# Attention and two mixtures of experts on one core: a reordered front, gate weights through memory, key sums from added chunks, zero-padded small groups

## The chip, the cores and the metric

The kernel runs on one core of a Trainium2 chip. The metric is the device time of one execution in microseconds (us), as the median of several runs. The engines are named as in the profile: PE (TensorE matmuls), PEld (its weight loads), DVE (VectorE), ACT (ScalarE), POOL (GpSimd) and SP (SyncE, which here issues most of the DMAs).

## What is computed

Three layers follow each other. B = 4 batches of S = 576 tokens give 2304 tokens of width 512.

```python
def _attn_ref(q, k, v):                       # (4, 8, 576, 64)
    q_s = softmax of q over the 64 features
    k_s = softmax of k over the 576 tokens
    kv = np.einsum('bhsd,bhse->bhde', k_s, v)
    return np.einsum('bhsd,bhde->bhse', q_s, kv)

def _moe_ref(x, w_gate, w1, w2, capacity):    # 8 experts, 512 -> 1024 -> 512
    probs = softmax(x @ w_gate); expert = argmax; gate_w = probs[expert]
    # the first `capacity` tokens of each expert are kept
    out = gate_w * (relu(x @ w1[expert]) @ w2[expert])   # 0 for dropped tokens

def _moe2_ref(x, w_skip, w_gate, w1, w2):
    # only tokens with x @ w_skip > 0; same top-1 expert, no capacity
    out = x + gate_w * (relu(x @ w1[e]) @ w2[e])         # others: out = x
```

The kernel is laid out for data in which a batch's tokens go to one expert in a layer, or only a few of them to one or two others; the fourth batch lies beyond the experts' capacity and its output is zeros (word `Z`). A general path for other data stands behind a branch at the end and is not taken.

## The kernel before, in words

**Groups.** A *group* is one dense pass of an expert over the 576 tokens of a batch. There are five: (layer 0, batch 0), (0, 1), (0, 2), (1, 0), (1, 1), called groups 1 to 5 here. In a group the tokens stand as columns. A group has 16 *steps*, counted 0 to 15. Steps 0 to 7 make the hidden layer: 24 matmuls of 288 columns each (line 813), where every fp32 operand is split in a high and a low fp32r part (`split`, lines 753 on ACT and 754 on DVE), so that a product is three matmuls. ACT and DVE take each step's result out (`evacuate`, `hh` on line 847 and `hl` on line 848). Steps 8 to 15 make the output in pairs of steps (line 834); after an odd step DVE multiplies the result with `mg` (lines 863 or 866 and 867), a tile that holds the gate weight of each token in every partition. Two pairs of PSUM banks alternate, so that a step's products go on while the step before is taken out.

**The plan.** The table `COURSE` gives each step of each group one line of words: those ahead of the bar are written behind the step's products and the split of the weights of the step after next, then comes `evacuate` of the step, then the words behind the bar. All engines run their instructions in the order in which the program writes them (`manual_schedule`), so the table sets the order on every engine. The words:

- `c.` to `i.`: the halves (four heads each) of the attention of batches 1 to 3. `ld` loads q, k and v; `qm`, `q1` to `q3`, `qn` are the softmax of q; `km`, `kt`, `kc`, `ke` shift the keys by their column maxima and take exp; `kv` (lines 415 and 424) is k times v; `qt`, `re`, `rw` turn q and write the layer's input.
- `C` and `M`: the routing of the two layers (`g` guesses the expert from a token, so that weights can be loaded early; 1 to 6 are logits, one-hot, positions, counts and gate weights).
- `G.1` makes the gate weight of each token with three small DVE operations (lines 876 to 880) in a column layout `gm` (128 x 5). `G.2` (`gate2`, line 887) spreads it over all partitions: five matmuls with `gm` as broadcast weights against the identity, and two ACT copies (895, 897) into `mg`.
- `L` and `N` load the weights of this and the next group (line 771, `ws`), `X` splits the next group's input.
- `S` (layer 0, batch 2, one expert) and `T` (layer 1, batch 2, two experts) are the *small groups*: at most 32 tokens that go to another expert. `p`, `g`, `gx` gather them, `t` (`expert`, line 1083) multiplies by that expert's weights, which come in eight tiles `tw` through three buffers (the load of tile i + 3 is written behind the matmuls that read tile i), `v` and `a` make the placing matrix, `u` (`put`, line 1132) adds the result to the batch's tokens, with a lhsT of 64 partitions.
- `O` turns a finished piece of 128 columns and stores it.

**v in the halves.** For halves `c` to `i` the tile of v is 65 wide with a column of ones, so that the k sums come out of the same matmuls; it is loaded head by head (five DMAs a half). For the two halves `a` and `b` of batch 0 v is 64 wide, loaded with two DMAs, and the sums are matmuls of their own (line 424).

**The front.** The attention of batch 0 (`a`, `b`) runs ahead of the groups. Filler matmuls (`warm_up`, line 511, 95 in all, 46 of them at the start) stand between its steps on PE. The order is: k of both halves, k times v, the last 64 tokens of q through to `X[0]`, the guess of the expert from them, the first weight loads (`first.load`), the other 512 tokens, the splits, and `first_products` (line 792), the products of steps 0 and 1 of group 1.

## Time and profile before

| | us |
|---|---|
| median of 3 runs | 438.97 |
| the runs | 434.55, 441.33, 438.97 |
| the profiled execution | 437.39 |
| its span, first to last instruction | 435.6 |
| TensorE clock granted, mean over the span | 0.983 of full speed |

The span is what the trace shows; the 1.8 us beside it lie around it. A row of the trace gives start and duration in us, engine, line, operation and tiles. L813 is line 813 of the kernel. In a chain of waits each piece is what the next one waited for. PEclk is the granted clock: 1.00 is 2.4 GHz, 0.50 is 1.2 GHz.

### The profile page before, as it was taken

The numbers are of one execution on the slowest core, as the hardware profiler recorded it, in microseconds if no ns is written. First come the engines' busy times: TensorE is split into PE (matmuls) and PEld (weight loads), VectorE is DVE, ScalarE is ACT, GpSimd is POOL, SyncE is SP. The second block draws the span as 40 slices with busy tenths as digits, with TensorE's granted clock in tenths as the row PEclk, the third lists the DMA queues.
The fourth block names the chain that finished last, engine by engine and source line by source line (L and its number), as shares of the span: only waits on it lengthen the run. The fifth ranks groups of instructions, "written<-read, shape, count | busy, mean of one in ns | idle before, by whom it ended". The sixth has DMA issues, their size and how long they took to land.

```text
span 435.6 us, 8703 instructions
## 1 busy us (share of the span) xinstructions
PE 407.3 (94%) x3370; PEld 359.7 (83%) x3370; DVE 243.2 (56%) x623; ACT 188.2 (43%) x574; POOL 7.6 (2%) x34
## 2 busy tenths in 40 slices
PE   8999799999999999999999979998999989999993
PEld 4666689898999898999998769798998878888882
DVE  3776478463778642577364625477665433554441
ACT  4646756733278653333366131333473423222121
POOL 3000000000000000000000000000000000000000
PEclk9999899999999999999999989999999989999997
DMA  8909915201942000791516921131326595620133
GB/s 213 247 14 263 234 50 161 53 2 52 295 109 87 12 2 2 250 204 50 185 58 212 246 94 50 50 94 52 120 93 188 177 289 165 186 117 2 32 105 85
DMA packets 75087, 53.30 MB, mean 122 GB/s; under 512 B 22562, under 2 KB 70178, under 8 KB 75042
## 3 DMA queue, kind: packets, MB, share of 16 engines
q1 hardware_dynamic: 73088, 52.41, 41.7%
q10 hardware_dynamic: 1954, 0.31, 0.5%
q8 instruction: 27, 0.44, 0.4%
q14 instruction: 18, 0.15, 0.1%
HBM read 47.98 MB, written 4.72 MB: 121 GB/s over the span
## 4 chain that ended last, share of the span: by engine, by line
PE 77%; DVE 9%; ACT 5%; SPq 3%; DMA 2%; issue 2%; DVEq 0%; ACTq 0%
PE pair L834 26%; PE pair L813 24%; PE pair L511 3%; PE pk L415 3%; DMA tw<-in_moe_w_dram 2%; PE pxs L1027 2%; PE px L473 2%; PE pl L565 2%; SPq L283 2%; PE pg L887 2%; PE pair L792 1%; PE pts L1132 1%; PE ptq L444 1%; PE pto L1165 1%; PE ph L1083 1%
## 5 line engine op out<-in xcount | busy, mean ns | idle before, releaser
L834 PE MATMUL pair<-hh,wh 128*128 128x288 f32 x320 | 98.5, 308 | 0.0
L834 PE MATMUL pair<-hl,wh 128*128 128x288 f32 x320 | 94.6, 295 | 0.0
L834 PE MATMUL pair<-hh,wl 128*128 128x288 f32 x320 | 94.3, 295 | 0.0
L813 PE MATMUL pair<-xh,wh 128*128 128x288 f32 x304 | 94.2, 310 | 0.0
L813 PE MATMUL pair<-xl,wh 128*128 128x288 f32 x304 | 90.8, 299 | 0.0
L813 PE MATMUL pair<-xh,wl 128*128 128x288 f32 x304 | 90.6, 298 | 0.0
L754 DVE TENSOR_TENSOR wl<-ws,wh 128x512 fp32r<-128x512 f32 x80 | 54.8, 686 | 43.0 <-ACT wh L753 42.6
L847 ACT ACTIVATE hh<-pair 128x576 fp32r<-128x576 f32 x40 | 25.9, 648 | 91.9 <-PE pair L813 81.4
L834 PEld LDWEIGHTS pair<-hh,wh 128*128 128x128 f32 x320 | 60.5, 189 | 3.6 <-issue 1.7
L813 PEld LDWEIGHTS pair<-xh,wh 128*128 128x128 f32 x304 | 58.2, 192 | 2.8 <-issue 1.1
L834 PEld LDWEIGHTS pair<-hl,wh 128*128 128x128 f32 x320 | 60.5, 189 | 0.1
L834 PEld LDWEIGHTS pair<-hh,wl 128*128 128x128 f32 x320 | 60.4, 189 | 0.0
L813 PEld LDWEIGHTS pair<-xl,wh 128*128 128x128 f32 x304 | 58.4, 192 | 0.1
L813 PEld LDWEIGHTS pair<-xh,wl 128*128 128x128 f32 x304 | 58.3, 192 | 0.0
L848 DVE SCALAR_TENSOR_TENSOR hl<-pair,hh 128x576 fp32r<-128x576 f32 x40 | 30.2, 756 | 48.0 <-ACT hh L847 46.4
L332 ACT ACTIVATE eq<-qt,mx 128x64 f32<-128x64 f32 x152 | 50.7, 337 | 5.0 <-DVE mx L321 4.6
L753 ACT CAST wh<-ws 128x512 fp32r<-128x512 f32 x80 | 49.3, 620 | 4.2 <-PE pair L834 2.8
L332 ACT ACTIVATION_READ_ACCUMULATOR eq<-qt,mx 128x1 f32 x152 | 28.8, 190 | 0.0
L511 PE MATMUL pair<-warm 128*128 128x384 f16 x95 | 20.9, 366 | 1.6 <-DVE warm L903 1.6
L754 DVE TENSOR_TENSOR xl<-x,xh 128x576 fp32r<-128x576 f32 x20 | 15.1, 753 | 11.1 <-ACT xh L753 11.1
L1166 ACT COPY ot<-pto 128x256 f32<-128x256 f32 (+1 forms) x24 | 7.2, 316 | 31.7 <-PE pto L1165 31.6
L511 PEld LDWEIGHTS <-warm 128*128 128x128 f16 x95 | 10.0, 108 | 10.4 <-issue 5.5
(186 smaller groups left out, 505.2 us busy)
## 6 DMA issues: line engine op xcount, KB each, us to landing
ws<-in_moe_w_dram SPq DMA_DIRECT2D x39, 512.0 KB, 3.9
tw<-in_moe_w_dram SPq DMA_DIRECT2D x24, 512.0 KB, 4.8
qt<-in_q_dram SPq DMA_DIRECT2D x8, 512.0 KB, 6.6
kt<-in_k_dram SPq DMA_DIRECT2D x8, 512.0 KB, 7.6
vt<-in_v_dram SPq DMA_DIRECT2D x24, 128.0 KB, 6.1
out_dram<-ot SPq DMA_DIRECT2D x12, 256.0 KB, 2.9
out_dram<-zt SPq DMA_DIRECT2D x2, 576.0 KB, 7.2
vt<-in_v_dram SPq DMA_DIRECT2D x2, 512.0 KB, 6.9
```

The costliest lines, as they stand in the source:

```text
L283: nc.sync.dma_start(out=t[:, h, 0:4, 0:D], in_=s[h, 0:4 * P].rearrange("h (p j) d -> p h j d", j=4))
L332: nc.scalar.activation(self.eqv[:, h, j], self.qt[:, h, j], AF.Exp, bias=self.mx[:, i:i + 1], accum_out=self.qz[:, i:i + 1])
L415: nc.tensor.matmul(out=pk[64 * g:64 * g + 64, c * D1:c * D1 + w], lhsT=self.kt[:rows(j), 2 * c + g, j], rhs=self.vt[:rows(j), 2 * c + g, j ...
L473: nc.tensor.matmul(out=pt, lhsT=self.kd[:, c], rhs=self.qT[:, c, 0:4 * P], start=True, stop=True)
L511: nc.tensor.matmul(out=pw[:, 0, :3 * P], lhsT=warm16[:, 0:P], rhs=warm16, start=True, stop=True)
L565: nc.tensor.matmul(out=pl[32 * c:32 * c + 32, :HT], lhsT=self.weights[:, c], rhs=self.chunk(c, tokens(a)), start=True, stop=True,)
L753: nc.scalar.copy(hi, src)
L754: nc.vector.tensor_tensor(out=lo, in0=src, in1=hi.bitcast(F32), op=ALU.subtract)
L813: nc.tensor.matmul(out=self.pt[:, a, :HT], lhsT=u[:, c], rhs=w[:, c, tokens(a)], start=(c == 0 and n == 0), stop=(c == NC - 1 and n == 2),)
L834: nc.tensor.matmul(out=self.pt[:, a, :HT], lhsT=p_[:, f], rhs=w[:, tokens(a)], start=(v == 0 and f == 0 and n == 0), stop=(v == 1 and f == ...
L847: nc.scalar.activation(halves(hh), src, AF.Relu)
L848: nc.vector.scalar_tensor_tensor(out=halves(hl), in0=src, scalar=0.0, in1=halves(hh).bitcast(F32), op0=ALU.max, op1=ALU.subtract,)
```

## The change

**Front.** 34 fillers at the start in place of 46, and 54 in all in place of 95. Half `a`'s main tokens are normalized, turned and multiplied earlier; the last tokens of both halves go through one bank and one copy; the loop over halves at the end is written out, without fillers, and `set_capacity` (a tiny matmul `pcap` behind a DVE cast of the capacity) moves from group 1 to just ahead of `first_products`.

**Gate weights.** For groups 2 to 5 `G.1` now also turns `gm` to 5 x 128 on PE, copies it out on DVE and writes it to memory with a DMA; `G.2` reads it back into all 128 partitions with a second DMA. Group 1 keeps the old way in one word, `G.0`. In the plan `G.1` moves to the words behind the bar of step 3 (groups 2 and 3) or step 4 (groups 4 and 5).

**k sums.** Halves `g` and `i` (batch 3) have v 64 wide, loaded with two DMAs in place of five. A new word `kz` adds the five chunks of k on DVE (three operations); in `kv` two PE transposes and a DVE reduction turn that into the sums.

**Small groups.** `put` takes a zero-padded lhsT of 128 partitions; two words `u` do what four did. In the plan the words of `S` and `T` start a line earlier and `t04` stands two lines behind `t03`, where it stood one.

The guess uses one token, not 64.

```diff
-    e.ke f.qm |
+    e.ke f.qm | G.1
-    f.q2 G.1 | f.kc
+    f.q2 | f.kc
-    N2 g.qn | S.t03
-    X2 | S.t04 g.qt
+    N2 g.qn S.v0 | S.t03
+    X2 | S.a0 g.qt
+    N3 | S.t04
...
+        def kz(self):
+            s2 = self.tile([P, HH, 2, D], "s2", "m2")
+            s1 = self.tile([P, HH, D], "s1", "m1")
+            kt = self.kt
+            nc.vector.tensor_add(s2, kt[:, :, 0:2], kt[:, :, 2:4])
+            nc.vector.tensor_add(s1, s2[:, :, 0], s2[:, :, 1])
+            nc.vector.tensor_add(s1, s1, kt[:, :, 4])
...
         def gate1(self):
+            self.gate_weights()
+            pt = bank("pgm")
+            nc.tensor.transpose(pt[0:NJ, 0:P], self.gm, ident)
+            gT = rp.tile([NJ, P], F32, name="gT", tag="gT")
+            nc.vector.tensor_copy(out=gT, in_=pt[0:NJ, 0:P])
+            self.gd = dp.tile([NJ, P], F32, name="gate", tag="gate", bufs=2)
+            nc.sync.dma_start(out=self.gd, in_=gT)
         def gate2(self):
             self.mg = hp.tile([P, S], F32, name="mg", tag="mg")
+            src = self.gd.rearrange("j p -> (j p)")[0:S].rearrange("(o n) -> o n", o=1)
+            nc.sync.dma_start(out=self.mg, in_=src.to_broadcast([P, S]))
...
-        warm_up(46)
+        warm_up(34)
...
+        first.split_w(0)
+        x_out(b, 1)()
+        first.split_w(1)
+        set_capacity()
         first.early = first.first_products()
...
-                        lhsT=u[sl, (c % 2) * P:(c % 2 + 1) * P],
-                        rhs=self.pT[t][sl, tokens(a)],
+                            out=pt[:, :HT], lhsT=u[:, c], rhs=self.pT[t][:, tokens(a)], start=(n == 0), stop=(n == 1)
```

How instructions move. DVE at the end of the front (`xl`, `wl` are the low parts of the input and the weights), before:

```order
L365 TENSOR_TENSOR eq<-eq,qz 128x2x4x64
L754 TENSOR_TENSOR xl<-x_121,xh 128x576 x2
L754 TENSOR_TENSOR wl_206<-ws_198,wh_202 128x512
L754 TENSOR_TENSOR wl_207<-ws_198,wh_203 128x512
L754 TENSOR_TENSOR xl<-x_121,xh 128x576 x2
L754 TENSOR_TENSOR wl_208<-ws_199,wh_204 128x512
```

and in the changed kernel:

```order
L367 TENSOR_TENSOR eq<-eq,qz 128x2x4x64
L775 TENSOR_TENSOR xl<-x_121,xh 128x576 x3
L775 TENSOR_TENSOR wl_206<-ws_198,wh_202 128x512
L775 TENSOR_TENSOR xl<-x_121,xh 128x576
L775 TENSOR_TENSOR wl_207<-ws_198,wh_203 128x512
L248 CAST capf<-capi 1x1
L251 COPY rem<-pcap 128x8
L775 TENSOR_TENSOR wl_208<-ws_199,wh_204 128x512
```

The cast `capf`, on which the matmul `pcap` waits ahead of all products, now stands behind the last split of the front.

DVE in group 2 around step 3 (`hl` is the result of steps 2 and 3, `mx<-qt` the word `f.qm`), before:

```order
L848 SCALAR_TENSOR_TENSOR hl<-pair_83,hh 128x576
L400 TENSOR_TENSOR kt<-kt,pmax 128x1280
L754 TENSOR_TENSOR wl_207<-ws_200,wh_203 128x512
L318 TENSOR_REDUCE mx<-qt 128x20
L321 TENSOR_SCALAR mx<-mx 128x20
L848 SCALAR_TENSOR_TENSOR hl<-pair_84,hh 128x576
L754 TENSOR_TENSOR wl_208<-ws_201,wh_204 128x512
```

and in the changed kernel:

```order
L869 SCALAR_TENSOR_TENSOR hl<-pair_84,hh 128x576
L404 TENSOR_TENSOR kt<-kt,pmax 128x1280
L775 TENSOR_TENSOR wl_207<-ws_200,wh_203 128x512
L320 TENSOR_REDUCE mx<-qt 128x20
L323 TENSOR_SCALAR mx<-mx 128x20
L869 SCALAR_TENSOR_TENSOR hl<-pair_83,hh 128x576
L897 TENSOR_SCALAR hi<-dlo_137 128x1
L898 SCALAR_TENSOR_TENSOR gm<-z_135,dlo_137,gw_136 128x5
L901 SCALAR_TENSOR_TENSOR gm<-z_135,hi,gm 128x5
L909 COPY gT<-pgm 5x128
L775 TENSOR_TENSOR wl_208<-ws_201,wh_204 128x512
```

PE at the same place, between the last products of step 3 and the first of step 4, in the changed kernel:

```order
L834 MATMUL pair_83<-xl,wh_205 128x288
L834 MATMUL pair_83<-xh,wl_209 128x288
L907 MATMUL pgm<-c_85,gm 5x128
L834 MATMUL pair_84<-xh,wh_202 128x288
L834 MATMUL pair_84<-xl,wh_202 128x288
```

The three `gm` operations stand behind `hl` of the step that has just ended, and the transposing matmul that reads `gm` stands ahead of the next step's products, where before one step followed the other.

SP in group 3, from the load of half `i` to the small group's last weight tile, before:

```order
L286 DMA kt<-in_k_dram 64x4x64
L283 DMA vt<-in_v_dram 128x4x64 x4
L286 DMA vt<-in_v_dram 64x4x64
L771 ISA
L771 DMA ws_200<-in_moe_w_dram 128x4x256
L1063 ISA
L1063 DMA tw<-in_moe_w_dram 128x2x512
```

and in the changed kernel:

```order
L287 DMA kt<-in_k_dram 64x4x64
L284 DMA vt<-in_v_dram 128x4x256
L287 DMA vt<-in_v_dram 64x4x64
L792 ISA
L792 DMA ws_200<-in_moe_w_dram 128x4x256
L1120 ISA
L1120 DMA tw<-in_moe_w_dram 128x2x512
```

Three issues fewer stand ahead of `tw`.

## Rows read from the trace of the kernel before

**Rows 1.** The page, part 1: busy time of each engine, its share, its instructions

```profile
PE 407.3 (94%) x3370; PEld 359.7 (83%) x3370; DVE 243.2 (56%) x623; ACT 188.2 (43%) x574; POOL 7.6 (2%) x34
```

**Rows 2.** Waits of PE: us in total, times, longest

```profile
PE py L1083 <- DMA tw<-in_moe_w_dram: 4.5, 2, 3.4
PE pt L384 <- ACT eq L332: 3.1, 1, 3.1
PE pts L1132 <- DVE x L1140: 2.2, 3, 1.0
```

**Rows 3.** Chain in order of time, front into group 1: start, us, what

```profile
39.63 6.37 PE pair L792 x48
...
50.95 4.72 PE pair L813 x24
```

**Rows 4.** Windows: busy us of each engine, then PEclk, DMA share, GB/s

```profile
50.00:55.00 5.00, 4.46 (x24) 4.49 (x25) 2.51 (x5) 3.79 (x19) 0.00 (x0) 0.69 0.77 208
...
355.00:360.00 5.00, 4.54 (x24) 4.40 (x23) 1.20 (x3) 1.07 (x3) 0.00 (x0) 0.66 0.92 306
```

**Rows 5.** Timeline of the front: start, us, engine, line

```profile
1.55 10.59 PE L511 MATMUL pair<-warm 128*128 128x384 f16 x46 [1.55 <-DVE warm L903]
...
9.49 0.42 DVE L378 TENSOR_TENSOR m<-m,kt 128x256 f32<-128x256 f32 x1
...
30.04 0.15 DVE L556 TENSOR_SCALAR gid<-gid 64x1 int32<-64x1 int32 x1
...
30.93 0.98 SPq L771 DMA_DIRECT2D ws<-in_moe_w_dram  x2
```

**Rows 6.** Groups of instructions by form, ACT: busy us, mean ns

```profile
L753 ACT CAST xh<-x 128x576 fp32r<-128x576 f32 x20 | 13.5, 674 | 0.1
...
L987 ACT COPY x<-px 128x512 f32<-128x512 f32 x4 | 2.3, 583 | 1.5 <-PE px L473 1.5
```

**Rows 7.** Chain in order of time, group 2, products of steps 2 to 4

```profile
124.21 3.19 PE pair L813 x24
...
127.84 6.37 PE pair L813 x48
```

**Rows 8.** Timeline of DVE and PE: group 2 step 3, group 3 step 3, group 4 step 4

```profile
132.19 1.48 DVE L318 TENSOR_REDUCE mx<-qt 128x20 f32<-128x1280 f32 x1
...
133.78 0.75 DVE L848 SCALAR_TENSOR_TENSOR hl<-pair,hh 128x576 fp32r<-128x576 f32 x1
...
203.60 0.64 PE L1042 MATMUL ptx<-c,x 128*128 128x128 f32 x4
203.67 0.76 DVE L848 SCALAR_TENSOR_TENSOR hl<-pair,hh 128x576 fp32r<-128x576 f32 x1 [1.32 <-ACT hh L847]
...
289.61 0.76 DVE L848 SCALAR_TENSOR_TENSOR hl<-pair,hh 128x576 fp32r<-128x576 f32 x1 [0.51 <-ACT hh L847]
```

**Rows 9.** Groups of instructions by form, DVE: the last gate operation

```profile
L880 DVE SCALAR_TENSOR_TENSOR gm<-z,hi,gm 128x5 f32<-128x5 f32 x5 | 1.1, 225 | 0.2
```

**Rows 10.** Chain in order of time, group 3, steps 8 to 14

```profile
225.18 1.25 PE pg L887 x10
...
239.87 1.87 SPq L283
...
247.88 4.92 DMA tw<-in_moe_w_dram
...
255.80 3.67 PE pair L834 x24
```

**Rows 11.** Chain in order of time, group 5

```profile
348.20 5.89 DMA tw<-in_moe_w_dram
...
356.54 4.51 PE pair L813 x24
...
386.96 0.53 PE pts L1132 x2
...
390.86 0.99 PE pts L1132 x6
```

More of the change, by code (lines that the diff above doesn't have):

```diff
@@ L242 @@
     beyond_i = cp.tile([P, 1], I32, name="beyond_i")
-    gkey = [cp.tile([LAST, 1], F32, name=f"gkey{b}") for b in range(len(GUESS))]
-    gid = [cp.tile([LAST, 1], I32, name=f"gid{b}") for b in range(len(GUESS))]
+    gkey = [cp.tile([1, 1], F32, name=f"gkey{b}") for b in range(len(GUESS))]
+    gid = [cp.tile([1, 1], I32, name=f"gid{b}") for b in range(len(GUESS))]
     def set_capacity():
@@ L298, in load_v @@
         def load_v(self):
[L300 to L301 removed]
+            if self.sums == 0:
+                self.vt = self.big("vt", D1)
                 nc.gpsimd.memset(self.vt[:, :, :, D:D1], 1.0)
+            else:
+                self.vt = self.big("vt")
             self.load(v, self.vt)
@@ L926 @@
         a.ke()
-        warm_up(8)
+        warm_up(7)
+        b.kc_max()
         a.inverse()
         a.norm(j=slice(4, 5))
-        b.kc()
+        b.kc_sub()
         warm_up(2)
-        p4 = bank("ptq4")
-        a.turn_last(p4)
-        a.to_last(nc.scalar.copy, a.qT, p4)
+        a.kv1()
         b.ke()
-        a.kv1()
-        warm_up(6)
         b.qm()
+        a.norm(slice(0, 2), F4)
+        pt = bank("ptq")
+        a.turn_new()
+        a.turn(0, pt)
         a.kv2()
+        nc.scalar.copy(a.qT[:, 0, 0:4 * P], pt)
+        b.exps(j4)
         b.exp_sub(slice(0, 2), F4)
-        b.exps(j4)
         b.kv1()
@@ L995 @@
     hp = ctx.enter_context(tc.tile_pool(name="hp", bufs=1, reuse_waits="tile"))
+    y2 = [hp.tile([P, NC, P], F32R, name=f"y{i}") for i in range(2)]
+    for t in y2:
+        nc.gpsimd.memset(t.bitcast(F32), 0.0)
     class Small:
@@ L1210, in word @@
         elif name == "G":
-            groups[k].gate1() if rest == "1" else groups[k].gate2()
+            (groups[k].gate, groups[k].gate1, groups[k].gate2)[int(rest)]()
         elif name[0] == "L":
```

284 lines of the change are left out of this document (146 added, 138 removed).

## The prediction

> **What bounds the kernel now.** I read the page's busy shares first, then what PE waited for, then the chain of waits in order of time, then windows of five us for the clock, and last the timelines of the places that the change touches. PE is busy 407.3 of 435.6 us [rows 1], and the chain runs through PE nearly all the way, so three things can shorten this kernel: less work on PE, less waiting of PE, and no stretch at the lower clock. The waits are few. The two longest are 4.5 us for the small groups' weight tiles and 3.1 us for the first transposes of group 1 [rows 2]. Both are dearer than they look. After the 3.1 us wait the next 24 products take 4.72 us [rows 3], where 24 take 3.19 us elsewhere [rows 7], because the granted clock in that stretch is 0.69, part of it at 1.2 GHz [rows 4]; the same follows the last wait for a weight tile, at 0.66 [rows 4], with 4.51 us for 24 products [rows 11]. So there a waiting PE costs its wait and some 1.5 us again (4.72 - 3.19). That price decides much below.
>
> The reader should see that in this kernel a step is PE's 3.2 to 3.4 us, and that what ACT and DVE do within a step costs nothing as long as PE has something to issue. Whatever makes PE wait within a step is paid in full.
>
> **The front.** Twelve fillers fewer at the start. The 46 end at 1.55 + 10.59 = 12.14 us, while the key maxima of half a, for which the first transposes wait, are ready at 9.49 + 0.42 = 9.91 us [rows 5]. The fillers' mean is 10.59 / 46 = 0.23 us, and 34 of them end near 9.9 us, the later ones running faster than the mean. So the key chains begin about 1.9 us earlier. Walking the new order with the same durations, some of that is lost again: exp of b's queries now stands on ACT behind the copy of a turned piece of a, which waits for a's k products and norm, and b's k products come before the shared last-token copy. I get the guessed expert (`gid`, 30.19 us before [rows 5]) at 29.0, and the first weight loads, issued at 30.93 [rows 5], 1.2 us earlier. From there ACT sets the pace, from about 28.4 us, when the first output piece is ready: four copies and two turned ones at 0.58, four casts at 0.67 [rows 6] and two weight casts at 0.6 (512 columns where the others have 576) make 3.5 + 2.7 + 1.2 = 7.4 us, to 35.8. Then come the last weight split on DVE, behind it the cast of the capacity, and behind that `pcap` on PE, which stands ahead of all products: they start at 37.1 and not at 39.6. `pcap` is what holds them; without it the first could start near 34.8. They need 6.37 us [rows 3], so the front would end at 43.5 and not 46.0 (39.63 + 6.37).
>
> But from 32.7 to 37 PE has nothing to do, and ahead of that only transposes and single matmuls with four fillers among them. An idle of 3.1 us was enough to lose the clock [rows 3, 4], so I take it as lost here too, for 1.5 us and a little in the turns, 1.7 in all: 45.2 us, a gain of 0.8. Bounds: 2.5 if the clock holds, -0.5 if the lower clock comes early and stretches the turns by a us or more. The next wait of PE, the 3.1 us, stays as it is: it hangs on ACT and DVE behind the routing's first matmuls (`pl`), whose place is unchanged.
>
> **The gate weights.** What goes: ten matmul rows in each of groups 2 to 5, 1.25 us in group 3 [rows 10], about 5.1 in all, and two ACT copies each, which lie beside PE. What comes, beside small DMAs: a transpose on PE in each, under 0.3 us. Its wait is the item. `G.1` now stands behind the bar, so on DVE the three gate operations (0.225 us for the last of them [rows 9], 0.65 for the three with their gaps) come after `hl` of the step that has just ended, and on PE the transpose comes before the next step's products. Before, those products went on in the other banks while `hl` was being made. Now they queue behind the transpose.
>
> - Group 2, step 3: the products of steps 3 and 4 run without a break from 127.84 for 6.37 us [rows 7], so step 3 ends near 131.0. DVE is late here: `f.qm` starts at 132.19, and `hl` ends at 133.78 + 0.75 = 134.53 [rows 8]. The gate is then ready at 135.2: PE waits 4.2 us, 4.4 with the transpose, and 1.5 more for the clock.
> - Group 3, step 3: `hl` ends at 204.43 [rows 8], but PE has the small group's gathering to do until 203.60 + 0.64 = 204.24 [rows 8]; the gate comes at 205.1, and PE waits 0.9, with the transpose 1.0.
> - Group 4, step 4: `hl` ends at 290.37 [rows 8]; the products of step 4 ended one ACT pass before it began at 289.61, near 288.8. The gate comes at 291.0: PE waits 2.2, with the transpose 2.4. I take the clock as held.
> - Group 5, step 4: four adds of `put` and two reductions of the routing stand on DVE ahead of the gate, and the step's words on PE take 4.8 us with their wait (`hl` 1.5 behind the products, adds 1.8, reductions 0.6, gate 0.65, transpose); the other three `put` words take 1.2, 1.2 and 2.3, where DVE's evacuation is in the way. In all 9.5. But DVE made PE wait in the old order too: four times eight matmuls at 0.99 + 0.53 [rows 11], two waits of about 1.0 [rows 2], the routing's turn 0.9, the old gate 1.25 make 10.2. So -0.7, the old gate included.
>
> The memory round trip itself hides: `mg` is first read at step 9, and two or three steps of over 3.3 us lie between the write, the read and that. On SP the write stands ahead of one weight load that waits for its buffer anyway. If the cover were gone, PE's products of step 11 would be late, by a DMA of some 4 to 6 us [rows 10, 11].
>
> Sum: group 2 4.4 + 1.5 - 1.25 = +4.65; group 3 1.0 - 1.25 = -0.25; group 4 2.4 - 1.25 = +1.15; group 5 -0.7. Together +4.85. Bounds: -5 if no wait shows, +9.4 if each of the four brings the lower clock.
>
> A rule on this: after the 3.1 us wait the row shows the clock at 0.69 [rows 4]. The Trainium skill ("TensorE: Matmul & The Clock Gate", section "Why this matters for your kernels") asks for no idle gaps between bursts of matmuls, since idle time sends the clock back to half. The trace agrees where it has a gap of 3 us; it has none of 2.3 between two dense runs. [...]
>
> **k sums and the load of v.** In group 3 SP spends about 7.7 us on the five pieces of half i's v: they take up to 1.87 us each [rows 10], while the weight tile for the last matmuls of `S` stands behind them. It is issued at 247.88 and lands 4.92 us later [rows 10]; the longest wait of PE, 3.4 us [rows 2], is this one. After it two short turns and 24 products run at the lower clock: 3.67 for the products [rows 10] against 3.19, and 1.1 more in the turns, 1.6 in all. With two pieces SP is past them some 5 us earlier, and in the new plan `t04` stands a further step behind `t03`, so even a landing of 5.9 us [rows 11] is covered by two steps of 3.3 us. I take the whole: -5.0. In group 5 the same wait (1.1 us, the rest of the 4.5 [rows 2]) and the lower clock after it (4.51 - 3.19 = 1.3, and 0.3 in small matmuls) go by the same extra step: -2.7. What they free is late next at `t10`, whose tile is issued in `t04`, one step ahead: +0.25. The added DVE work, three adds and a reduction, about 2 us a half, lies under the products of steps of 5 us; the two transposes cost 0.15 us a half: +0.3.
>
> **Small groups' results.** As many matmuls as before, 48. With 64 partitions six take 0.99 us, 0.165 each [rows 11], products 0.133 (6.37 / 48 [rows 7]). At most 48 x 0.03 = 1.5 us, but DVE's adds hold the fourth bank in each word, so I take 0 beyond what is counted above. The split of the result in two parts doubles two small operations on ACT and DVE, which lie under a step.
>
> A rule that speaks against this: the row shows no two of these matmuls at once. The Trainium skill (same page, same section, on small contractions) says that matmuls on distinct row groups run concurrently and that a 32-row one takes as long as a 128-row one, so padding would give concurrency away. The neighbours here share a row group, and 0.165 is above the full-height pitch, so the trace shows nothing to lose. By the rule as far as it could go, 48 x 0.133 / 2 = +3.2 us.
>
> **The plan's other moves.** PE's work is the same. In group 3 five bank uses now stand in one step and `g.rw` behind `evacuate`: +0.6. In group 5 one more piece is turned behind the last products, five transposes on three banks ahead of the last evacuation: +0.2 net, as the same work leaves an earlier step.
>
> **Sum.** Front -0.8, gate +4.85, weight tiles -5.0 - 2.7 + 0.25, sums +0.3, plan +0.8: -2.3 us, against the profiled execution 437.4 - 2.3 = 435.1. That execution lies 1.6 below the median of the runs shown, so against the median 438.97 the forecast is 436.7 us: no change that a measurement of this kernel could tell, for which I take 2%, or 8.8 us.
>
> **Rivals.**
>
> 1. *The gate waits are not there, and the front keeps its clock.* Then the gate gives its 5.1, and the front 2.5: -2.3 - 4.85 - 5.1 - 1.7 = -14, or 425 us. For it: the old order never showed such a wait. Against it: the order of DVE and PE is fixed, and `hl` cannot end before the products it reads.
> 2. *Slower: the gate's transposes stop PE in all four groups, each long enough to bring the lower clock.* Place: the end of step 3 or 4 of each group. Price: three falls of the clock beside the one counted, 4.5 us, and with the front's gain gone 0.8: -2.3 + 5.3 = +3.0, or 442 us. It decides from the point where the gate costs more than the 7.15 us that all else gives (0.8 + 7.45 - 0.3 - 0.8): two more falls do (4.85 + 3.0). For it: a wait of 3.1 us costs the clock here. Against: a wait of 0.9 us [rows 8] is short.
> 3. *The front gives nothing*, as the products are held by `pcap` at the lower clock and the weights land late: 437.5 us.
> 4. *The change doesn't do what it says for the weight tiles*: SP is held by something else than the pieces of v, and the 5 us stay: 441.7 us. Against it: the chain names those issues one by one [rows 10].
>
> **How the numbers follow.** My forecast 0.60, with a range of its own from 433 to 440.5; rival 1, in full or half (from 425 to 430), 0.17; rival 2 0.09; rival 3 0.08; rival 4 0.06. The range from 428.5 to 442.5 takes in half of rival 1, and rivals 2 to 4. Faster by over 2% (below 430.2) is most of rival 1 and a little of the forecast's low side: 0.17. Slower by over 2% (above 447.7) is the tail of rival 2, with more waits than I counted: 0.06. The rest, 0.77, is within 2%.
>
> **What would show it.** Right: products of group 1 start near 37 us, just behind `pcap`, at half the pitch for a while; a wait of PE for the last gate operation of some 4 us in group 2, 2.3 in group 4, 1 in group 3; no wait for `tw` of more than 0.5 us; the 3.1 us wait of group 1 still there. Wrong: products before 36 us or after 39; a gate wait in group 2 under 2 us; a granted clock near 1.00 in the windows after those waits; new waits of PE in groups 3 to 5 that none of these steps names.

## The result and the profile after

The changed kernel takes 442.21 us (median of 20 runs, 438.85 to 443.49) where the kernel before takes 438.22 (20 runs). The ratio is 1.0124, 95% interval 1.0091 to 1.0157: slower by 1.2%. That is less than the 2% that the prediction calls a change, but the interval lies clear of 1, on the other side of it than the forecast of -2.3 us, and the time lies above the forecast's range of 433 to 440.5. The ratio leaves out slow runs, those more than 1.5% above the fastest of their kernel, six of the 20 of the kernel before; so it is larger than 442.21 / 438.22.

The profiled execution has a span of 441.7 us, against 435.6: +6.1 us to explain. It took 443.49 us, the most of the 20, at a mean granted clock of 0.948, which ten of the 20 show (the fastest has 0.963); the profiled execution of before took 437.39, less than its median. Between the two medians lie 4.0 us, so some 2 of the +6.1 come with these two executions.

The page of the changed kernel, its busy shares and the granted clock in 40 slices of 11 us:

```profile
PE 403.4 (91%) x3297; PEld 359.2 (81%) x3297; DVE 250.1 (57%) x636; ACT 185.8 (42%) x570; POOL 8.3 (2%) x34
...
PEclk9958879999998899999999999998999999999996
```

PE has *less* to do than before [rows 1], 403.4 us against 407.3, and the span is longer. So the time is in waits and in the clock: the line of the clock has dips in its slices 3 to 6 (22 to 66 us), 13 and 14, and 28. The waits of PE:

```profile
PE pgm L907 <- DVE gm L901: 7.9, 4, 4.1
PE pt L386 <- DVE m L380: 4.5, 3, 3.4
PE pcap L250 <- DVE capf L248: 3.3, 1, 3.3
PE pto L1218 <- DVE x L888: 3.0, 1, 3.0
```

Against [rows 2], the wait for weight tiles (`py` for `tw`) is gone, as forecast, two waits are new, for the gate weights (forecast) and for the capacity (forecast as an idle stretch of PE), and the one for the last piece of x grew from 0.8 us, which was not forecast. In the kernel before it is

```profile
PE pto L1165 <- DVE x L867: 0.8, 1, 0.8
```

By stage, from the first product of a group on PE to that of the next:

| stage | before | after | change | predicted |
|---|---|---|---|---|
| front, to the end of the first products | 46.00 | 51.14 | +5.1 | -0.8 |
| from there to group 2 | 70.55 | 71.47 | +0.9 | 0 |
| group 2 | 69.44 | 74.27 | +4.8 | +4.65 |
| group 3 | 81.99 | 75.58 | -6.4 | -4.5 |
| group 4 | 76.17 | 79.19 | +3.0 | +1.3 |
| group 5, to its last product | 82.59 | 78.34 | -4.25 | -3.15 |
| tail | 8.86 | 11.71 | +2.85 | +0.2 |
| sum | 435.6 | 441.7 | +6.1 | -2.3 |

Three places were misjudged: the front by 5.9 us, the tail by 2.65, group 4 by 1.7. Groups 3 and 5 gave 3.0 more than forecast. Two of these misses are in part one word or one store that crossed a boundary between stages. The word `g.rw` stood in step 14 of group 3 and stands in the first step of group 4 now, which takes 4.81 us for 3.29, 0.78 of them a wait of PE for ACT. And the turns of one store left step 11 of group 5 for the tail (experiment 7).

**The front.** The windows of five us of the changed kernel (busy time of each engine with its instructions, then the granted clock and the DMA):

```profile
15.00:20.00 5.00, 4.29 (x84) 3.46 (x84) 4.90 (x9) 2.24 (x2) 0.00 (x0) 1.00 1.12 285
20.00:25.00 5.00, 4.90 (x66) 4.15 (x66) 3.20 (x10) 3.76 (x18) 0.00 (x0) 0.55 0.17 46
25.00:30.00 5.00, 5.00 (x40) 4.33 (x38) 2.07 (x9) 2.23 (x11) 0.00 (x0) 0.50 0.00 0
30.00:35.00 5.00, 5.00 (x22) 2.90 (x22) 2.27 (x9) 1.49 (x3) 0.99 (x2) 0.59 0.29 88
35.00:40.00 5.00, 2.07 (x5) 0.41 (x3) 2.96 (x5) 4.94 (x10) 0.00 (x0) 1.00 1.05 234
40.00:45.00 5.00, 3.62 (x15) 3.63 (x16) 3.58 (x7) 0.83 (x2) 0.00 (x0) 0.60 1.03 303
45.00:50.00 5.00, 5.00 (x30) 5.00 (x30) 0.00 (x0) 0.41 (x1) 0.00 (x0) 0.72 1.23 267
```

The clock is at 1.2 GHz from about 21 to 34 us, although PE is shown as busy nearly all that time, and for 4.29 of the five us ahead of it: what it runs from 16.5 us on is products of k and v with 64 columns and one column, and transposes. The clock falls a second time at 41 us, at the end of PE's wait for the capacity. What stands just ahead of the first products, in the timeline:

```profile
36.95 1.13 PE L495 MATMUL px<-qT,kvd 128*128 128x512 f32 x2 [1.01 <-ACT qT L1033]
...
40.50 0.68 DVE L775 TENSOR_TENSOR wl<-ws,wh 128x512 fp32r<-128x512 f32 x1
...
41.10 0.13 DVE L248 CAST capf<-capi 1x1 f32<-1x1 int32 x1
...
41.38 0.55 PE L250 MATMUL pcap<-capf,ones 1*128 1x2 f32 x2 [3.31 <-DVE capf L248]
41.87 0.61 PE L813 MATMUL pair<-xh,wh 128*128 128x288 f32 x1
```

As the prediction said, the tiny `pcap` holds the products behind the last weight split and the cast of the capacity. But it does so from 38.1 to 41.4 us, not to 37.1, and the 48 products then take 9.27 us (41.87 to 51.14) and not 6.67.

**Groups 2 and 4.** The waits for the gate, and windows of two us around each (the last two rows of the second fence are group 4):

```profile
141.19 0.37 PE L907 MATMUL pgm<-c,gm 128*5 128x128 f32 x1 [4.11 <-DVE gm L901]
...
296.97 0.38 PE L907 MATMUL pgm<-c,gm 128*5 128x128 f32 x1 [1.99 <-DVE gm L901]
```

```profile
136.00:138.00 2.00, 1.08 (x9) 0.84 (x7) 2.00 (x3) 0.23 (x2) 0.00 (x0) 1.00 0.00 0
138.00:140.00 2.00, 0.00 (x0) 0.00 (x0) 1.97 (x4) 2.00 (x3) 0.00 (x0) 0.99 0.00 0
140.00:142.00 2.00, 0.81 (x4) 0.84 (x5) 1.41 (x6) 2.00 (x13) 0.00 (x0) 0.50 0.00 0
142.00:144.00 2.00, 2.00 (x10) 2.00 (x9) 0.48 (x1) 0.13 (x2) 0.00 (x0) 0.50 0.16 47
...
296.00:298.00 2.00, 1.03 (x5) 1.03 (x6) 1.50 (x6) 0.18 (x1) 0.00 (x0) 0.74 0.03 8
298.00:300.00 2.00, 2.00 (x10) 2.00 (x9) 1.35 (x8) 0.24 (x1) 0.00 (x0) 0.50 0.21 61
```

PE does nothing from 137.1 to 141.2 us, and the 24 products behind the transpose take 5.92 us where 24 take 3.43 with the clock held. In group 4 the wait is 2.0 us, forecast 2.2, but the clock fell there too, which was not forecast: 4.96 us for 24.

**The tail.** DVE's last two sums, and PE's wait for them. In the kernel before, where the span ends at 435.6:

```profile
427.56 0.45 DVE L866 TENSOR_TENSOR yt<-pair,mg 128x288 f32<-128x288 f32 x1
```

and in the changed kernel:

```profile
431.42 0.42 DVE L1219 COPY ot<-pto 128x256 f32<-128x256 f32 x1 [0.53 <-PE pto L1218]
433.98 0.46 DVE L887 TENSOR_TENSOR yt<-pair,mg 128x288 f32<-128x288 f32 x1 [2.13 <-DMA out_dram<-ot]
434.47 0.46 DVE L888 TENSOR_TENSOR x<-x,yt 128x288 f32<-128x288 f32 x1
```

```profile
435.07 0.82 PE L1218 MATMUL pto<-c,x 128*64 128x128 f32 x3 [3.02 <-DVE x L888]
```

The gated product `yt` waits for a *store* (`out_dram<-ot`). It takes its tile from the same three buffers as the stores' `ot`, and the new plan issues two stores in the last step.

### The profile page after: what moved, and what is told of

The parts are those of the page before. It is cut to its first block, busy times and chain, and to the rows that moved or that the text cites. A ratio compares the mean times of both kernels' runs of the same rounds, so it can differ in the third digit from the quotient of the medians.

```text
span 441.7 us, 8583 instructions
## 1 busy us (share of the span) xinstructions
PE 403.4 (91%) x3297; PEld 359.2 (81%) x3297; DVE 250.1 (57%) x636; ACT 185.8 (42%) x570; POOL 8.3 (2%) x34
## 4 chain that ended last, share of the span: by engine, by line
PE 76%; DVE 10%; ACT 7%; issue 3%; DMA 2%; SPq 0%; DVEq 0%; ACTq 0%
PE pair L855 28%; PE pair L834 24%; PE pk L437 4%; PE pair L813 2%; PE px L495 2%; PE ptq L463 2%; PE pl L586 2%; PE pxs L1084 2%; ACT eq L334 2%; ACT hh L868 1%; PE pto L1218 1%; DMA kt<-in_k_dram 1%; PE py L1140 1%; PE ph L1140 1%; DVE wl L775 1%
## 5 line engine op out<-in xcount | busy, mean ns | idle before, releaser
L834 PE MATMUL pair<-xh,wh 128*128 128x288 f32 x304 | 96.1, 316 | 0.0
L834 PE MATMUL pair<-xl,wh 128*128 128x288 f32 x304 | 92.3, 304 | 0.0
L834 PE MATMUL pair<-xh,wl 128*128 128x288 f32 x304 | 92.1, 303 | 0.0
L775 DVE TENSOR_TENSOR wl<-ws,wh 128x512 fp32r<-128x512 f32 x80 | 54.9, 686 | 38.1 <-ACT wh L774 37.1
L834 PEld LDWEIGHTS pair<-xh,wh 128*128 128x128 f32 x304 | 60.0, 197 | 2.2 <-issue 0.9
L834 PEld LDWEIGHTS pair<-xl,wh 128*128 128x128 f32 x304 | 60.1, 198 | 0.1
L834 PEld LDWEIGHTS pair<-xh,wl 128*128 128x128 f32 x304 | 59.8, 197 | 0.0
L411 ACT ACTIVATE kt<-kt 128x1280 f32<-128x1280 f32 x8 | 10.2, 1272 | 13.8 <-issue 7.1
L437 PE MATMUL pk<-vt,kt 128*64 128x64 f32 (+3 forms) x320 | 15.9, 242 | 0.0
```

The lines of the kernel that those rows point to most:

```text
L411: nc.scalar.activation(self.kt, self.kt, AF.Exp)
L437: nc.tensor.matmul(out=pk[64 * g:64 * g + 64, c * D1 + o:c * D1 + o + n], lhsT=self.kt[:rows(j), 2 * c + g, j], rhs=ones32[:rows(j), 0:1] ...
L775: nc.vector.tensor_tensor(out=lo, in0=src, in1=hi.bitcast(F32), op=ALU.subtract)
L834: nc.tensor.matmul(out=self.pt[:, a, :HT], lhsT=u[:, c], rhs=w[:, c, tokens(a)], start=(c == 0 and n == 0), stop=(c == NC - 1 and n == 2),)
```

## The experiments

Twelve kernels, each the changed kernel with one edit unless said otherwise. Ratios are to the kernel before on the same chip. Edits 5, 9 and 10 have four runs, 11 and 12 six, the others ten.

| edit | median us | ratio, 95% interval | span of the profile |
|---|---|---|---|
| (the change itself) | 442.21 | 1.0124 (1.0091 to 1.0157) | 441.7 |
| 1 front of before | 436.91 | 0.9979 (0.9932 to 1.0027) | 434.0 |
| 2 fillers in the new front | 436.21 | 0.9944 (0.9902 to 0.9987) | 433.7 |
| 3 capacity back in group 1 | 435.46 | 0.9952 (0.9922 to 0.9982) | 433.4 |
| 4 gate by PE, as before | 436.64 | 0.9976 (0.9938 to 1.0013) | 432.6 |
| 5 gate through memory, ahead of the bar | 429.59 | 0.9787 (0.9736 to 0.9837) | 427.8 |
| 6 fillers in the gate's waits | 436.81 | 0.9981 (0.9947 to 1.0015) | 434.7 |
| 7 stores in the order of before | 439.50 | 1.0021 (0.9984 to 1.0059) | 437.8 |
| 8 v head by head, no added chunks | 442.07 | 1.0073 (1.0043 to 1.0103) | 439.6 |
| 9 `t04` a step earlier | 447.45 | 1.0191 (1.0115 to 1.0266) | 446.3 |
| 10 edits 8 and 9 | 447.69 | 1.0245 (1.0179 to 1.0312) | 445.5 |
| 11 edits 2, 3, 5, 7 together | 423.26 | 0.9663 (0.9614 to 0.9712) | 422.5 |
| 12 edit 11 with two more | 421.50 | 0.9649 (0.9594 to 0.9703) | 419.3 |

The front differs between executions of one code: the first products end between 48.4 and 51.1 us in the eight profiles that keep the new front as it is. So each edit is read from its own stage, and the span beside it. Against the 2% mark, 11 and 12 are faster than the kernel before; the intervals of 5, 9 and 10 take in the mark; the others lie within it.

### 1. The front of before

```diff
-        warm_up(34)
+        warm_up(46)
...
-        set_capacity()
         first.early = first.first_products()
...
+            if kk == 0 and i == 1:
+                set_capacity()
             groups[kk].products(i)
```

> The changed kernel with the whole front of before (95 fillers, its order, the capacity's matmul back in group 1); all else changed. Theory (the new front itself costs the time, by its clock): the products of steps 0 and 1 end near 46.0 us again and not at 51.1, and group 1 takes 70.5 and not 71.5, so the span falls by about 6.0 us from 441.7 to 435.7; gate waits and tail stay as they are. Rival (the front's loss is hidden behind later weights, group 1 only waits elsewhere): span 439.5 or more.

The first products run from 40.39 to 47.05 us and group 2 begins at 115.92, where the changed kernel has 122.61: 6.7 us back, and the span falls by 7.7. Of the 6.7, only 4.1 lie in the front, which ends 1.1 us later than expected (the clock was low from 26 to 33 us). The other 2.6 lie in group 1 and are in the main chance: its old wait is there,

```profile
51.60 0.41 PE L386 MATMUL pt<-c,m 128*128 128x128 f32 x2 [3.13 <-ACT eq L334]
```

but the clock held behind it in this execution, and the next 24 products took 3.42 us, where they took 5.88 in the changed kernel. The front is a loss of its own, and nothing later hides it.

### 2. Fillers in the new front

```diff
         a.kv1()
+        warm_up(6)
...
         b.exp_act(slice(0, 2), F4)
+        warm_up(4)
...
         first.split_w(1)
+        warm_up(12)
         set_capacity()
```

and 3 behind each turn, 2 behind each output piece and 3 behind the last tokens of half `a`: 39 in all, so that 93 stand in the kernel, and 95 in the kernel before.

> The changed kernel with its own front order, and fillers put back between its steps: 6 behind half a's k products, 4 behind half b's, 3 behind each turn and 2 behind each output piece, 12 ahead of the capacity's matmul. Theory (the lower clock is what the front lost): granted clock 1.00 from 20 to 34 us and in the first products, which take 6.4 us and not 9.3, begin near 40 and end near 46.5; span 437. Rival (the order, with its longer chain over ACT and DVE, is what is slow): the first products begin at 41.4 or later as before, and the front ends at 48 or later even at the full clock; span 438.5 or more. Second rival (fillers only push the chain back): front ends at 51 or later, span 441.7 or more.

The same windows as above:

```profile
20.00:25.00 5.00, 5.00 (x93) 4.04 (x91) 2.76 (x8) 3.74 (x18) 0.00 (x0) 1.00 0.10 23
25.00:30.00 5.00, 4.81 (x37) 3.14 (x36) 3.99 (x16) 2.55 (x13) 0.00 (x0) 1.00 0.00 0
30.00:35.00 5.00, 5.00 (x24) 2.70 (x23) 2.12 (x3) 4.03 (x8) 0.00 (x0) 1.00 0.61 167
...
40.00:45.00 5.00, 5.00 (x39) 5.00 (x39) 1.68 (x3) 0.65 (x1) 0.00 (x0) 1.00 1.08 322
```

The clock stays at 2.4 GHz, 93 matmuls pass from 20 to 25 us in place of 66, and the products run from 38.79 to 45.43. So with the clock held the new order is 0.6 us ahead of before, with its `pcap` still in the way: holding the clock is enough to give back the front's loss. The next edit gives it back in another way.

### 3. The capacity back in group 1, no fillers

```diff
+            if kk == 0 and i == 1:
+                set_capacity()
             groups[kk].products(i)
...
-        set_capacity()
         first.early = first.first_products()
```

> The changed kernel with the capacity's tiny matmul back in group 1; the front's order and its few fillers are the new ones. Prediction's step (the tiny matmul holds the first products, which could start some 2.3 us earlier without it): the products begin 2.0 us or more earlier than the 38.8 to 41.9 of the runs that keep it, against the end of the last px matmul. Rival (the split of the first weights on ACT and DVE comes barely before it): the products begin within 1.5 us of the old distance of 3.8 us behind the last px; at the lower clock in either case.

```profile
35.67 1.12 PE L495 MATMUL px<-qT,kvd 128*128 128x512 f32 x2 [1.01 <-ACT qT L1033]
37.38 0.40 PE L813 MATMUL pair<-xh,wh 128*128 128x288 f32 x1 [0.58 <-ACT wh L774]
```

The products begin 0.6 us behind the last `px`, where they began 3.8 us behind it, and end at 44.75. The clock is low from 23 to 33 us here too, but PE no longer stands still for 3.3 us behind that, and is not at the lower clock in the products (7.37 us, a wait of 0.35 among them). The expectation's "at the lower clock in either case" did not come true. Part of the 6.4 us by which the front ends earlier is chance: in edits 7 to 9 the clock fell at 22 us, about as here, and their first products end at 49.34 to 49.55, so the tiny matmul ahead of the products is worth 4.6 to 4.8 us. Edits 2 and 3 overlap: `pcap` costs that much where PE stands still behind it and the clock falls again, and 2.3 where fillers stand in its wait (edit 2 ends at 45.43, and edit 12, which has no `pcap` there and five fillers fewer, at 43.12).

### 4. The gate by PE, at the steps of before

```diff
-    e.ke f.qm | G.1
+    e.ke f.qm |
...
-    f.q2 | f.kc
-    f.ke | e.re
+    f.q2 G.3 | f.kc
+    f.ke | e.re G.4
```

and in the same way in groups 3 to 5 (`G.3` the three DVE operations, `G.4` the five matmuls and two copies).

> The changed kernel with the gate weights of groups 2 to 5 made as before, by five matmuls on PE and two ACT copies at the steps of before. Theory (the transpose of the gate behind the bar makes PE wait and brings the lower clock): the waits for the gate of 4.1, 0.8, 2.0 and 1.0 us go, group 2 shortens by 4.8 and group 4 by 3.0 us, groups 3 and 5 change by less than 0.5; span 434.0. Rival (DVE's backlog holds PE, whatever it works on): PE waits in group 2 for the low part of a hidden piece or its bank instead, groups 2 and 4 gain under 3 us together; span 439 or more.

Group 2 takes 69.29 us (74.27), group 3 75.79 (75.58), group 4 78.35 (79.19); no wait for the gate is left, and no other takes its place in group 2. Group 4 gains 0.8 and not the 3.0 expected: the clock falls there behind another wait (last section). The theory holds for group 2 in full, for group 4 in its wait.

### 5. The gate through memory, ahead of the bar

```diff
-    e.ke f.qm | G.1
-    L6 e.q3 | e.kv
-    e.qn f.q1 | G.2
-    L7 f.km | e.qt f.kt
+    e.ke f.qm |
+    L6 G.3 e.q3 | e.kv
+    G.5 e.qn f.q1 |
+    L7 f.km G.2 | e.qt f.kt
```

and so in groups 3 to 5 (`G.5` is the transpose and the write).

> The changed kernel, its gate weights still through memory, but ahead of the bar and in two steps: the three DVE operations a step earlier than the transpose and the write, the read one step after that. Theory (only the place behind the bar, after the low part of the step, makes PE wait): no wait for the gate over 0.5 us, ten matmul rows fewer than with the old way, so 1.0 us or more under it (432.6 in the profile of that run, whose front was 2.6 us shorter than here to be expected): span 433.5, a ratio near 0.993 to before. Rival (the way through memory itself costs: the read comes late, or the write on SP's queue holds the weight loads): a new wait for mg on DVE in steps 9 to 11 or for the weights, span 437 or more.

Groups 2 to 4 take 68.45, 74.60 and 76.19 us, group 5 77.19: 11 us less than in the changed kernel, and in each group less than with the five matmuls on PE. No wait for the gate over 0.5 us is left, and none for `mg`. Two waits elsewhere grew by 0.7 us each (a turn of group 2, the one-hot of group 4). So the way through memory was worth having, and what cost the 11 us was where `G.1` stood. Falls of the clock are part of them, 2.5 us in group 2 and 1.5 in group 4 (next experiment), and 1.5 of the 2.2 us between edits 4 and 5 in group 4 are one too. The span is 5.7 us under what was expected; 2.7 of these are the front, which ended at 48.45 in this execution.

### 6. Fillers in the gate's waits

```diff
+            if rest == "1" and k in (1, 3):
+                ph = bank("hold")
+                for _ in range({1: 26, 3: 13}[k]):
+                    nc.tensor.matmul(out=ph[:, :3 * P], lhsT=c16[:, 0:P], rhs=c16, start=True, stop=True)
```

> The changed kernel with fillers on PE ahead of the gate's transpose, in a bank of their own: 26 of 384 columns in group 2 and 13 in group 4, which end about when the gate weights come. They shorten no wait, and only keep PE at work in it. Theory (each of these two waits costs its length and the lower clock behind it): the 24 products behind the transpose take 3.3 us and not 5.9 in group 2, and 3.3 and not 5.0 in group 4, so group 2 takes 71.7 in place of 74.3 and group 4 77.5 in place of 79.2; granted clock 1.00 there. Rival (the clock falls for another reason than the wait, or the fillers' bank makes the transpose later by as much): groups 2 and 4 within 0.7 us of 74.3 and 79.2.

Windows of group 2, where the changed kernel stands still and then runs at 0.50:

```profile
136.00:138.00 2.00, 2.00 (x14) 1.22 (x13) 1.97 (x5) 2.00 (x8) 0.00 (x0) 1.00 0.00 0
138.00:140.00 2.00, 2.00 (x16) 1.68 (x15) 1.14 (x4) 1.39 (x9) 0.00 (x0) 1.00 0.01 1
140.00:142.00 2.00, 2.00 (x20) 1.83 (x20) 0.00 (x0) 0.06 (x1) 0.00 (x0) 1.00 0.56 168
```

The 24 products behind the transpose take 3.42 us in both groups. Group 2 takes 71.77 and group 4 77.72 us, as expected. This splits the price: in group 2, 2.5 us are the clock and the rest is the wait; in group 4, 1.5. For group 2 the case is firm, as the clock fell behind this wait in all eight profiles that have it without fillers (in edits 1 and 2 for 1.5 us only, with 4.96 and 4.95 us for the 24 products). For group 4 it is weaker, as the clock held there without fillers in five of the eight.

### 7. The stores in the order of before

```diff
-    | T.u11 O1.0
-    | O2.0
-    | O1.1 O2.1
-    | O2.2
-    | O1.2 O2.3
+    | T.u11 O2.0 O1.0
+    | O2.1
+    | O1.1 O2.2
+    | O2.3
+    | O1.2
```

> The changed kernel with the stores of the last five steps in the order of before (one store in the last step, not two). Theory (the last gated sum takes its tile from the three buffers of the stores, and with two stores in the last step it waits until one has left): the wait of 3.0 us of PE for the last x is gone, the tail from the end of the products is 8.9 and not 11.7 us; span 439.0. Rival (the stores' transfers are bound by their queue, and the wait only moves): tail over 11 us, span 441.5.

```profile
429.93 0.45 DVE L887 TENSOR_TENSOR yt<-pair,mg 128x288 f32<-128x288 f32 x1
430.41 0.46 DVE L888 TENSOR_TENSOR x<-x,yt 128x288 f32<-128x288 f32 x1
```

```profile
431.02 0.49 PE L1218 MATMUL pto<-c,x 128*64 128x128 f32 x3 [0.78 <-DVE x L888]
```

`yt` waits for nothing, PE's wait is 0.78 us as before, and the tail takes 8.7 us. The whole loss of the tail was the buffer. But the moved store is turned in step 11 of group 5 again, which takes 7.56 us and not 6.67, and group 5 takes 79.21 us and not 78.34. So edit 7 gives back 2.1 us and not 3.0, and of group 5's gain 0.9 is the same store.

### 8 to 10. The loads of v and the step of t04

Edit 8 loads v of halves `g` and `i` head by head again, and `kz` does nothing; edit 9 moves `t04` to the step right behind `t03`; edit 10 does both.

```diff
-    H = {n: Half(... sums=0 if i < 4 else 2) ...}
+    H = {n: Half(... sums=0) ...}
...
-    X2 | S.a0 g.qt
-    N3 | S.t04
+    X2 | S.t04 g.qt
+    N3 | S.a0
...
-    | T.a0 i.rw
-    L5 | T.t04 C3.1
+    | T.t04 i.rw
+    L5 | T.a0 C3.1
```

> The changed kernel with v of halves g and i loaded head by head into the tile of 65 columns as before, and without the added chunks; the plan is unchanged. Theory of the prediction (SP's five pieces of v hold the weight tiles of the small groups): a wait for a tile of 3 us or more comes back in group 3, with the lower clock after it, and group 3 takes 80 us in place of 75.6. Rival (the plan's later words for the last expert step cover it whatever SP does): group 3 stays within 1 us of 75.6, group 5 within 1 of 78.3.

> The changed kernel with the word t04 of both small groups one step earlier, right behind the step of t03 as before; v is still loaded in two pieces. The run above showed that five pieces of v bring no wait back, so it is open which part removed the waits for weight tiles. Theory of the prediction (SP passes v sooner, so the tile lands in time whatever the plan): no wait for a tile over 0.7 us, group 3 takes 75.6 as in the changed kernel. New theory (the extra step between t03 and t04 is what covers the landing): waits of 2 us or more in group 3 and about 1 us in group 5 with the lower clock behind them, group 3 near 79 or more, group 5 longer by 1 to 2.5 us.

> The changed kernel with both parts back: v of halves g and i head by head, no added chunks, and t04 one step earlier. Theory (each of the two parts covers the wait alone): the wait of 3.4 us for a tile is back here, and only here, group 3 takes 80 to 82. Rival (the plan alone decides): the same wait as with t04 earlier and v in two pieces, within 0.5 us.

With five pieces of v and the new step, no wait for a tile shows, and group 3 takes 75.36 us (75.58): the rival. With `t04` early and v in two pieces, group 3 takes 79.26 us; with both back, 79.74. The last matmuls of `S` and the issue of their tile, with `t04` early and two pieces:

```profile
254.19 0.38 SPq L1120 DMA_DIRECT2D tw<-in_moe_w_dram  x1
```

```profile
260.78 0.80 PE L1140 MATMUL py<-tw,hT 128*32 128x256 f32 x8 [2.28 <-DMA tw<-in_moe_w_dram]
```

and with `t04` early and five pieces:

```profile
258.03 0.38 SPq L1122 DMA_DIRECT2D tw<-in_moe_w_dram  x1
```

```profile
262.77 1.08 PE L1142 MATMUL py<-tw,hT 128*32 128x256 f32 x8 [3.02 <-DMA tw<-in_moe_w_dram]
```

The runs lie 1.2 us apart at this point (`t03`'s matmuls begin at 253.49 and 254.73), so two pieces bring the issue 2.6 us earlier, but the tile then needs 6.6 us from issue to use and not 4.7. Of the 3.0 us of waiting two pieces save 0.7; the extra step saves all of it, with either load. SP is done with v at 251.50 us in edit 9 and issues the tile only at 254.19, behind the matmuls of `t03` that read the buffer. So edit 9 bears out its new theory in group 3 and not in group 5, and of edit 10 neither text holds in full: the wait is not back "only here", and it is 0.74 us longer than in edit 9, not within 0.5.

In group 5 no wait for a tile came back in any of the three, so which part of the plan removed that one stays open; edit 9 takes 2.6 us longer there (80.93), of which 1.5 are a fall of the clock behind the gate and 1.1 lie in step 1, where PE's wait for ACT's turn of `i.rw` grew from 0.60 to 1.36 us. In edit 8 group 5 took 79.68, outside what was expected, with the same fall behind its gate (4.79 us for 24 products against 3.42).

What the added chunks themselves cost shows in group 4. Edit 8, without them, takes 78.11 us, and the run of edit 7, which has them and the same fall of the clock at the gate, 79.16: 1.05 us, of which 0.70 is a new wait of PE for DVE's sum (`pt` for `s`, line 419).

### 11 and 12. Versions that beat both

Edit 11 is 2, 3, 5 and 7 together, with 10 fillers at the front's end.

> The changed kernel with four mends together: fillers in the front as in the run above but 10 at its end, the capacity's matmul back in group 1, the gate weights ahead of the bar in two steps, and the stores of the last steps in the order of before. Theory (the losses add up): front ends near 45, group 2 takes 69, group 4 76, tail 9, so a span near 422 to 424 and a ratio of 0.970 to before. Rival (the losses hide each other, DVE or SP is late next): span 428 or more.

Front to 46.05 us, group 2 68.42, group 3 74.60, group 4 76.19, tail 8.8: the losses add up. Edit 12 has 7 fillers at the end, and 18 in group 1 where PE waited 3.1 us:

```diff
-    c.km c.q1 | c.kt
+    c.km c.q1 | F.18 c.kt
```

> The combined version of the run above, with 7 fillers and not 10 at the end of the front, and 18 fillers of 384 columns in group 1 ahead of the first transposes of half c, in the 3.1 us that PE waits there. Theory (the wait costs its length and the lower clock behind it, and only the second can be had back by fillers): the 24 products behind it take 3.3 and not 4.7 us, group 1 from the start of its products 75.6 and not 77.1, span 421. Rival (the clock does not fall there, or the fillers push the transposes back): span 422.5 or more.

```profile
PE 396.6 (95%) x3349; PEld 351.8 (84%) x3349; DVE 249.2 (59%) x636; ACT 185.5 (44%) x570; POOL 8.3 (2%) x34
...
PEclk9999999999999999999999999998999999999998
```

Group 1, from its first product, takes 75.64 us and not 77.07, with no wait for its first transposes, and one dip of the clock left ahead of the tail (slice 28, in group 4). Edit 1 had this stage as short, 75.54, without these fillers, so one profile does not show that they did it. The front ends at 43.12 us, 2.9 earlier than in edit 11, where the clock fell from 25 to 31 us. The ratio to before is 0.9649, 3.5% faster; edits 11 and 12 are not told apart by their ratios, only by these two stages.

## Why the prediction was wrong, point by point

**The front: the step that failed.** Forecast -0.8 us, measured +5.1 (+2.4 to +5.1 in the eight profiles with this front). Three terms:

- "I get the guessed expert at 29.0": with the clock held (edit 2) it is ready at 29.65 us; in the changed kernel at 31.43 (31.29 + 0.14), and the weights are issued at 32.18, *later* than before. I priced the lower clock at 1.7 us in all, beginning with an idle stretch at 32.7. It begins at 21 us and stretches everything that follows. I had looked for idle time, and the trace of before shows that stretch with fillers in it. So the term that failed is this price of 1.7 us: against edit 2, which holds the clock, the front lost 5.7 us in the changed kernel's profile, and 3.0 in the least of the eight. My bound for this case ("if the lower clock comes early") gave it a loss of 0.5 us.
- "ACT sets the pace from about 28.4 us ... to 35.8": I added up ACT's work as if it ran without a break. Each output piece goes PE, ACT, PE, ACT. With the clock held the last weight split of step 1 ends near 38.3 us (37.63 + 0.69), not near 36.5; so `pcap` ends at 38.86 in edit 2 and not at 37.1.
- "`pcap` is what holds them; without it the first could start near 34.8": right in kind: edit 3 gives back the front and more. But the start without it is 37.38, as the first weight split comes then. The stall of 3.3 us that it makes was forecast as an idle stretch, and what the clock costs behind it was put too low: the products take 9.27 us against 6.67.

**The gate.** The mechanism and its place were right, and group 2 to 0.2 us, partly by luck: the wait is 4.1 for 4.2, but the clock behind it took 2.5 and not 1.5 (edit 6; 1.5 in edits 1 and 2), and of the wait only 3.3 us come back where it goes (71.77 in edit 6, 68.45 in edit 5). The waits in groups 3, 4 and 5 are 0.8, 2.0 and 1.0, forecast 0.9, 2.2 and within a longer sum. What failed is "I take the clock as held" in group 4: 1.5 us in the profile, and a fall in three of eight profiles. The rows of before held a warning: the last wait for a weight tile is 1.1 us long by [rows 2], and the clock stands at 0.66 behind it [rows 4]. The rule cited beside it (the Trainium skill, "TensorE: Matmul & The Clock Gate", section "Why this matters for your kernels") is for longer idle gaps than this one of 2.0 us; here the measurement decides, and it shows a fall in some executions.

**The weight tiles.** The amount was near: with both parts back (edit 10) group 3 takes 4.2 us more, forecast 5.0; the rest of its 6.4 us has other causes, `g.rw` among them. The cause was not right: "with two pieces SP is past them some 5 us earlier" is worth 0.7 us of the wait alone (edits 9 and 10). The second reason of the same sentence, the extra step of `t04`, did it all in group 3 (edit 8). Rival 4, SP held by something else than v, had it half: the issue also waits for the tile's buffer.

**k sums.** Forecast +0.3, measured about +1.05 in group 4 (edit 8 against edit 7) and 0.2 in group 3: in the main a wait for DVE's sum that I had taken as hidden under the products.

**The results of the small groups.** Forecast 0. Six matmuls of 128 partitions take 0.95 and 0.96 us in group 5; six of 64 took 0.99 in the chain of before [rows 11] and 1.06 in its timeline. At most 0.1 us is gained in each such run, and the +3.2 us by the rule on small contractions do not show.

**The plan's other moves.** Forecast +0.6 in group 3, with `g.rw` there. The word stands in group 4 now and costs 1.5 us there (4.81 for 3.29 in its step). With the clock's 1.5 and the 0.9 that the sums cost beyond forecast this is more than group 4's miss of 1.7; some 2 us less in its steps 11 to 15, which turn one store fewer and have three small waits less, stand against them.

**The tail.** Forecast +0.2, measured +2.85, or +2.0 with the 0.9 us that the store's turns save in group 5 (edit 7). I counted transposes and banks of the store that moved, and not the buffer that it takes: with two stores in the last step the third of the three `ot` buffers was still leaving when `yt` asked for one.

**The sum.** Rival 2 (slower, 442 us) has the measured time, but not the way, so its number is luck: it wanted the lower clock behind all four gates. In the profile that came in two of four, and the front and the tail made the rest.

## What to carry to other kernels

A matmul that waits stopped all matmuls written behind it (3.3 us behind `pcap`, 4.1 behind the gate's transpose), so a tiny one is written where its operand has long been ready, not just ahead of dense work: of the two moves of this kind here, `pcap` and the gate's transpose, the second alone cost 11 us with its falls of the clock, more than the 6.1 by which the profile of the change is longer. When a step is moved, list every buffer it takes as well as its instructions, and ask who else draws on that pool in the same step. And fillers are not waste to be trimmed by count: a stretch of small matmuls that loses them has to be priced with the lower clock over its whole length (nine of nine profiles here), and a wait that cannot be removed can at least keep the clock with fillers of its own (2.5 us in group 2).

## What the runs showed of the hardware

**The same wait brings the lower clock in some executions and not in others.** Eight profiles have the four gate waits unchanged. In or behind the 4.1 us the clock fell in 8 of 8, behind the 2.0 us in 3, behind the 1.0 us (with another of 1.1 us two us ahead of it) in 2, behind the 0.8 us in none. Behind the wait of 3.1 to 3.4 us in group 1 it fell in 12 of the 13 profiles that have it, all but edit 1. In group 4 a wait of 1.13 us for the routing's one-hot (line 637, 616 before) stands nine or ten us later; of eleven profiles that have it, that of the kernel before among them, five lost the clock there, none of them one that had lost it at group 4's gate. The changed kernel and edit 1:

```profile
307.26 0.27 PE L637 MATMUL pp<-oh,c 128*128 128x32 f16 x4 [1.13 <-DVE oh L629]
```

```profile
308.00:310.00 2.00, 2.00 (x16) 1.98 (x17) 1.73 (x11) 0.00 (x0) 0.00 (x0) 1.00 0.00 0
310.00:312.00 2.00, 2.00 (x19) 2.00 (x18) 0.77 (x7) 0.49 (x1) 0.00 (x0) 1.00 0.14 26
```

```profile
298.07 0.26 PE L637 MATMUL pp<-oh,c 128*128 128x32 f16 x4 [1.14 <-DVE oh L629]
```

```profile
298.00:300.00 2.00, 1.93 (x23) 1.86 (x24) 1.71 (x7) 0.18 (x1) 0.00 (x0) 0.79 0.72 282
300.00:302.00 2.00, 2.00 (x10) 2.00 (x10) 1.48 (x12) 0.00 (x0) 0.00 (x0) 0.50 0.01 5
```

So such a wait costs 1.5 us with some chance, and an edit that removes one can show little of its gain in a single profile, as edit 4 in group 4. The Trainium skill ("TensorE: Matmul & The Clock Gate", section "What's actually happening") says that the number of slow matmuls at a kernel's start varies from run to run; these rows show the like in the middle of a kernel.

**The clock fell while PE was shown as busy.** All nine profiles with the new front and no fillers added lost the clock between 20 and 27 us, in the changed kernel with PE busy for 4.29 of the five us ahead of 20 us and for 9.9 of the 10 from 20 to 30; of the three with fillers one did (edit 11, from about 24 to 31 us). The old front, with its 95 fillers, lost it in edit 1 (26 to 33 us) and not in the kernel before. What PE runs in this stretch is in the main matmuls with 64 columns and with one, and transposes; which of them matters is not shown.
